# Attention and a softplus feed-forward on one core: products and TensorE sums issued for two key tiles at a time

## The chip, the cores and the metric

One core of a Trainium2 chip runs the whole program. The metric is device time in microseconds (us) from start to end of one execution; three runs of the kernel before gave 985.01, 985.25 and 985.94 us, median 985.25 us.

## The reference

For each of 4 batches and 8 heads there are 1152 keys and values of 64 numbers, and 576 queries, which are means of two neighbouring rows of `q`. Attention's output is the input of a two-layer feed-forward with a softplus between the layers.

```python
q_pool = q.reshape(B, H, S // 2, 2, D).mean(axis=3)
scores = scale * np.matmul(q_pool, k.transpose(0, 1, 3, 2))
attn = np.exp(scores - scores.max(-1)); attn /= attn.sum(-1) + 1e-09
x = np.matmul(attn, v)            # then (2304, 512): tokens by heads*64
h = x @ w_in                      # 512 -> 2048
g = np.maximum(h, 0.0) + np.log1p(np.exp(-np.abs(h)))
out = g @ w_out                   # 2048 -> 512
```

All of it is float32 at the ends. The kernel takes the large products of scores and feed-forward in float16 halves (a high part and a low part), and the product with the values and the sums of exponentials in float32.

## The kernel before

The work is cut into 16 units, `u0` to `u15`: a unit is one batch and two heads. A unit's 576 queries are taken in two halves, of 256 and 320 columns (`HALF`, `n`), and its 1152 keys in nine tiles of 128 (`KT`). For each half and each tile of keys, `attention` makes five kinds of work:

- **scores** (L777 and L780): four float16 matmuls, two for each head, into one of two PSUM buffers `s`;
- **exp** (L787): one ScalarE activation over both heads from `s` into one of four SBUF buffers `p`;
- **product** (L795): values times `p` for both heads into the one PSUM buffer `pv`. Each head takes 64 columns of the array. A float32 matmul of the program is two instructions in the trace, so one tile's product is 4 of them;
- **sums**: in units 0 to 5 (`SUMMED`) TensorE makes them (L802), with a matrix of ones and 32 columns of the array for each of four quarters, into the free end of `pv`, 8 instructions of the trace for one tile. In units 6 to 15 VectorE or GpSimd add the `p` tiles (L348) into `acc`, and TensorE sums over partitions once per half (`total`, L860);
- after the ninth tile: `pv` is copied out, the sums go through three small DMAs, `few`, `scratch` and `rinv` (L875, L880, L883), which turn them into one row of reciprocals for all partitions, and one multiplication finishes the half.

Ahead of a unit's attention, `maxima` computes its row maxima (L667 and L678 on TensorE, whose operands use 64 rows of the array, and reductions L688 on VectorE) and turns them (L713, L717). `feed_forward` does the first layer in blocks of columns (`unit`, L1009, then softplus on ScalarE, L1020), and the second layer in pieces of 12 matmuls (L960). Maxima, first and second layer share three PSUM buffers `m`.

The order of instructions on every engine is fixed when the program is built: each piece of work is a task with a price per engine, dependencies, a priority and buffers to take and give, and `Sched.run` plays the tasks through with those prices and lets each engine take the ready task of lowest priority number. On the chip, each engine then works in that order and waits where data isn't ready. In `attention` the scores of tile `kt` have priority `x.at + x.slow * (9 i + kt)`, the product that plus 1.9, the additions that plus 2.0. `ORDER` says which units and feed-forward blocks lie side by side: units 0 to 5 run nearly alone, from unit 6 on pieces of the second layer lie between attention's.

## Time and profile before

| | |
|---|---|
| median of three runs | 985.25 us |
| the profiled execution, its own time | 984.97 us |
| its span, first to last instruction | 983.3 us |
| TensorE (PE) busy | 903.1 us, 92% of the span |
| VectorE (DVE) busy | 608.3 us, 62% |
| ScalarE (ACT) busy | 472.4 us, 48% |
| GpSimd (POOL) busy | 162.8 us, 17% |
| mean granted TensorE clock | 0.979 of full speed |

Busy time is the union of an engine's instructions; a matmul's end is modelled, so what a block of matmuls takes is best read from the start of its first row to the start of the next row. A row of the timeline can hold several instructions (x8); its second column is how long they ran together. In brackets behind it stands how long the engine had been idle before, and who released it.

### The profile page before, as it was taken

To read this page: it belongs to the slowest core of one execution; us is meant where nothing else is said; L and a number is where in the kernel's file an instruction comes from. 1 tells how busy PE (TensorE), PEld (TensorE's weight loads), DVE (VectorE), ACT (ScalarE), POOL (GpSimd) and SP (SyncE) were. 2 spreads that over 40 slices of the span, in tenths; PEclk is the share of its full clock that TensorE was granted. 3 is DMA by queue.
4 is the path that set the end of the run, shared out by engine and by line. 5 is a ranking of instruction groups with operands and counts; after the bars stand their busy time and mean duration, and the time that the engine had idled before them with its cause. 6 is when DMAs were issued, how large, how long until landed. Compare 5 with 4: busy or idle time off the path is not lost.

```text
span 983.3 us, 16320 instructions
## 1 busy us (share of the span) xinstructions
PE 903.1 (92%) x6426; PEld 452.8 (46%) x6426; DVE 608.3 (62%) x1301; ACT 472.4 (48%) x739; POOL 162.8 (17%) x141
## 2 busy tenths in 40 slices
PE   2799999798789999999999999999899999969998
PEld 0244344244534456444544564333654744335483
DVE  5777587877667766666664467777654657526030
ACT  4547477777765345345442354455533545322020
POOL 1000010210212411134001112344112013000000
PEclk9999999799989999999999999999999999979999
DMA  8725426456434025041310151432300300000000
GB/s 239 189 81 152 124 78 190 115 170 162 123 94 104 12 62 90 12 136 37 68 37 28 43 96 39 107 78 68 86 1 17 91 1 17 13 18 1 22 12 21
DMA packets 101581, 74.61 MB, mean 76 GB/s; under 512 B 68480, under 2 KB 82816, under 8 KB 101504
## 3 DMA queue, kind: packets, MB, share of 16 engines
q1 hardware_dynamic: 101504, 73.57, 28.3%
q8 instruction: 50, 0.82, 0.4%
q14 instruction: 27, 0.22, 0.1%
HBM read 49.81 MB, written 4.79 MB: 56 GB/s over the span
## 4 chain that ended last, share of the span: by engine, by line
PE 54%; DMA 8%; DVE 7%; ACT 4%; issue 1%; POOL 0%; SPq 0%; ACTq 0%; DVEq 0%
PE m L960 16%; PE m L1009 14%; PE pv L795 10%; DMA rinv<-scratch 5%; PE s L777 5%; PE s L780 4%; PE m L667 3%; DVE nm L688 2%; DMA scratch<-few 2%; DMA few<-rinv 1%; ACT g L1020 1%; ACT p L787 1%; DVE xT L348 1%; ACT L787 1%; DVE w L275 1%
## 5 line engine op out<-in xcount | busy, mean ns | idle before, releaser
L787 ACT ACTIVATE p<-s,cols 128x512 f32<-128x512 f32 (+1 forms) x288 | 209.5, 738 | 209.3 <-PE s L780 206.8
L688 DVE TENSOR_REDUCE nm<-m 128x1 f32<-128x384 f32 x432 | 222.6, 550 | 108.9 <-PE m L667 100.3
L795 PE MATMUL pv<-p,v 128*64 128x320 f32 (+1 forms) x1152 | 207.1, 441 | 3.4 <-ACT rinv L868 1.6
L960 PE MATMUL m<-w,gh 128*128 128x512 f16 x576 | 171.8, 380 | 0.0
L777 PE MATMUL s<-qA,kT 128*128 128x256 f16 (+1 forms) x576 | 159.4, 296 | 8.5 <-ACT p L787 8.4
L780 PE MATMUL s<-qB,kB 66*128 66x256 f16 (+1 forms) x576 | 157.8, 293 | 0.0
L348 POOL TENSOR_TENSOR acc<-acc,p 128x512 f32<-128x512 f32 (+1 forms) x73 | 104.6, 1433 | 225.2 <-ACT p L787 189.8
L1009 PEld LDWEIGHTS <-w1h 128*128 128x128 f16 x1024 | 99.7, 99 | 49.7 <-issue 25.4
L960 PE MATMUL m<-w,gl 128*128 128x512 f16 x288 | 109.1, 379 | 0.0
L1020 ACT ACTIVATE g<-m,blk 128x512 f32<-128x512 f32 (+1 forms) x80 | 51.4, 642 | 110.1 <-PE m L1009 106.3
L1009 PE MATMUL m<-xh,w1h 128*128 128x256 f16 (+1 forms) x512 | 85.4, 289 | 17.7 <-DVE xh L272 7.7
L777 PEld LDWEIGHTS <-kT 128*128 128x128 f16 x576 | 57.8, 100 | 90.4 <-issue 80.6
L667 PE MATMUL m<-kT,qA 64*128 64x384 f16 x384 | 74.3, 347 | 20.2 <-DMA qA<-qcat 9.6
L795 PEld LDWEIGHTS pv<-p,v 128*64 128x64 f32 x1152 | 58.7, 137 | 72.2 <-issue 57.6
L960 PEld LDWEIGHTS <-gh 128*128 128x128 f16 x576 | 54.1, 98 | 68.0 <-issue 11.1
L1009 PE MATMUL m<-xl,w1h 128*128 128x256 f16 (+1 forms) x512 | 85.2, 290 | 0.0
L1009 PE MATMUL m<-xh,w1l 128*128 128x256 f16 (+1 forms) x512 | 84.8, 289 | 0.0
L348 DVE TENSOR_TENSOR acc<-acc,p 128x640 f32<-128x640 f32 (+1 forms) x67 | 50.8, 758 | 45.1 <-ACT p L787 36.9
L272 DVE TENSOR_SCALAR gh<-g,blk 128x512 f16<-128x512 f32 (+1 forms) x64 | 29.4, 459 | 76.4 <-ACT g L1020 76.1
L780 PEld LDWEIGHTS <-kB 66*128 66x128 f16 x576 | 57.3, 100 | 19.3 <-issue 9.3
L275 DVE SCALAR_TENSOR_TENSOR gl<-g,blk,gh 128x512 f16<-128x512 f32 (+1 forms) x80 | 55.7, 696 | 5.1 <-ACT gh L315 2.3
L667 PEld LDWEIGHTS <-qA 64*128 64x128 f16 x384 | 19.5, 93 | 85.2 <-issue 75.3
(139 smaller groups left out, 836.3 us busy)
## 6 DMA issues: line engine op xcount, KB each, us to landing
raw<-in_k_dram SPq DMA_DIRECT2D x16, 576.0 KB
v<-in_v_dram SPq DMA_DIRECT2D x16, 576.0 KB
raw<-in_q_dram SPq DMA_DIRECT2D x64, 128.0 KB
raw<-in_moe_w_out_dram SPq DMA_DIRECT2D x16, 512.0 KB
kB<-kT SPq DMA_DIRECT2D x32, 144.0 KB
gh<-in_moe_w_in_dram SPq DMA_DIRECT2D x4, 1024.0 KB
gl<-in_moe_w_in_dram SPq DMA_DIRECT2D x4, 1024.0 KB
out_dram<-o SPq DMA_DIRECT2D x16, 256.0 KB
```

The source lines that it names most:

```text
L272: nc.vector.tensor_scalar(out=out_, in0=in_, scalar1=s1, scalar2=s2, op0=op0, **kw)
L275: nc.vector.scalar_tensor_tensor(out=out_, in0=in0, scalar=s, in1=in1, op0=op0, op1=op1)
L348: e.tensor_tensor(out=o, in0=a, in1=b, op=op)
L667: nc.tensor.matmul(out=ps[h].item[:, 0:384], lhsT=x.qA.item[hs, PLACE[h, t]], rhs=x.kT.item[hs, k0:k0 + 3].rearrange("p a b -> p (a b)"), ...
L688: parts.append(task([("DVE", dve(384), lambda c=c, g=g, bank=bank: nc.vector.tensor_reduce(out=x.nm3.item[:, c, g:g + 1], in_=bank.item[:, ...
L777: nc.tensor.matmul(out=s.item[:, h, 0:n], lhsT=x.kT.item[:, h * KT + kt], rhs=x.qA.item.rearrange("p a b -> p (a b)")[:, c0:c0 + n], start ...
L780: nc.tensor.matmul(out=s.item[:, h, 0:n], lhsT=x.kB.item[0:D + 2, h * KT + kt], rhs=x.qB.item[0:D + 2, h, t0 * 64:t1 * 64], start=False, s ...
L787: nc.scalar.activation(out=pt.item[:, :, 0:n], in_=s.item[:, :, 0:n], func=ACTF.Exp, scale=x.sc)
L795: nc.tensor.matmul(out=pv.item[h * 64:(h + 1) * 64, 0:n], lhsT=x.v.item[:, h, kt], rhs=pt.item[:, h, 0:n], start=(kt == 0), stop=(kt == KT ...
L960: nc.tensor.matmul(out=ps.item[:, 0:512], lhsT=gt[:, f, t * 128:(t + 1) * 128], rhs=w2[:, f, wt, :], start=(f == 0 and m == 0), stop=(f == ...
L1009: nc.tensor.matmul(out=pv[:, f], lhsT=wt[:, kk, c0:c0 + 128], rhs=xt[:, kk, 0:w], start=(idx == 0), stop=(idx == 11))
L1020: x = task([("ACT", act(N, 1, 1), lambda: nc.scalar.activation(out=gs.item[:, 0:N], in_=ps.item[:, 0:N], func=ACTF.Softplus, scale=ih[:, g ...
```

## The change

The tiles of keys are put in five groups for each half: (0,1), (2,3), (4,5), (6,7) and (8). Scores and exp stay one task per tile, with the same buffers. The product is one task per group: it waits for both exponentials, then issues the sums of both tiles and the products of both tiles (products first in the group that begins at tile 0). Its priority is that of the group's first tile plus 2.8. The additions of units 6 to 15 get that priority too. Prices change: scores plus 60 instead of 30, products plus 220 or 140 per group instead of 160 or 80 per tile. In units 0 to 5 a `p` buffer now has one user to begin with, instead of two of which one is taken off at once.

```diff
--- before.py
+++ after.py
@@ -362,6 +362,7 @@
              "U6", "D6", "U7", "D7")
     SUMMED = range(6)
     STEPS = 2 * KT
+    GROUPS = [tuple(range(a, min(a + 2, KT))) for a in range(0, KT, 2)]
     blocks = []
     for b in range(B):
         if b % 2 == 0:
@@ -550,7 +551,7 @@
         x.kT, x.kB, x.qA, x.qB = (
             Hold(kT_r, 2 * KT + 15), Hold(kB_r, 2 * KT), Hold(qA_r, 2 * KT + 15), Hold(qB_r, 2 * KT))
         x.qlow = Hold(qlow_r, 3)
-        x.v = Hold(v_r, 2 * KT + 1)
+        x.v = Hold(v_r, 2 * len(GROUPS) + 1)
         x.sc = c[8]
 
 
@@ -765,69 +766,77 @@
         for i, (t0, t1) in enumerate(HALF):
             n = (t1 - t0) * 64
             pv, acc = Hold(pv_r), Hold(acc_r)
+            here = x.u in SUMMED
             before = None
             sums = None
-            for kt in range(KT):
-                prio = x.at + x.slow * (9.0 * i + kt)
-                s, pt = Hold(s_r), Hold(p_r, 2)
...
-                y = task([("PE", pe(4, n) + 30.0, scores)], [x.kB_done, x.q2_done, *x.qB_done[i]], prio, take=[s],
-                         give=[x.kT, x.kB, x.qA, x.qB])
...
-                e = task([("ACT", act(2 * n, 1, 1), exp)], [y, x.sc_done, *gate], prio, take=[pt], give=[s])
-                exps.setdefault(x.u, []).append(e)
...
-                def product_and_sums(kt=kt, product=product, summed=summed):
...
-                here = x.u in SUMMED
-                y = task([("PE", pe(1, (6 if here else 4) * n) + (160.0 if here else 80.0), product_and_sums if here else product)],
-                         [e, x.v_done], prio + 1.9,
-                         take=[pv] if kt == 0 else [], give=[pt, x.v])
...
-                    sums = task(tt_ways(2 * n, add, ALU.add), [e, before if kt == 1 else sums], prio + 2.0,
-                                take=[acc] if kt == 1 else [], give=[pt] + ([first] if kt == 1 else []))
-                    sums.price = {"DVE": 500.0}
-                before = e
+            first = done = None
+            for group in GROUPS:
+                prio = x.at + x.slow * (9.0 * i + group[0])
+                items = [(kt, Hold(s_r), Hold(p_r, 1 if here else 2)) for kt in group]
+                es = []
+                y = None
+                for kt, s, pt in items:
+                    def scores(kt=kt, s=s, t0=t0, t1=t1, n=n, i=i):
+                        for h in range(2):
+                            c0 = FIRST[h, i]
+                            nc.tensor.matmul(out=s.item[:, h, 0:n], lhsT=x.kT.item[:, h * KT + kt],
+                                             rhs=x.qA.item.rearrange("p a b -> p (a b)")[:, c0:c0 + n],
+                                             start=True, stop=False)
+                            nc.tensor.matmul(out=s.item[:, h, 0:n], lhsT=x.kB.item[0:D + 2, h * KT + kt],
+                                             rhs=x.qB.item[0:D + 2, h, t0 * 64:t1 * 64], start=False, stop=True)
+
+                    y = task([("PE", pe(4, n) + 60.0, scores)], [x.kB_done, x.q2_done, *x.qB_done[i]],
+                             x.at + x.slow * (9.0 * i + kt), take=[s], give=[x.kT, x.kB, x.qA, x.qB])
+
+                    def exp(s=s, pt=pt, n=n):
+                        nc.scalar.activation(out=pt.item[:, :, 0:n], in_=s.item[:, :, 0:n], func=ACTF.Exp,
+                                             scale=x.sc)
+
+                    es.append(task([("ACT", act(2 * n, 1, 1), exp)], [y, x.sc_done, *gate], prio, take=[pt],
+                                   give=[s]))
+                exps.setdefault(x.u, []).extend(es)
+
+                def products(items=items, pv=pv, n=n):
+                    for kt, _, pt in items:
+                        for h in range(2):
+                            nc.tensor.matmul(out=pv.item[h * 64:(h + 1) * 64, 0:n], lhsT=x.v.item[:, h, kt],
+                                             rhs=pt.item[:, h, 0:n], start=(kt == 0), stop=(kt == KT - 1))
+
+                def summed(items=items, pv=pv, n=n):
+                    for _, _, pt in items:
+                        for a in range(2):
+                            for h in range(2):
+                                g = 64 * h + 32 * a
+                                nc.tensor.matmul(
+                                    out=pv.item[g:g + 32, 512 - n // 2:512], lhsT=ones[:, 0:32],
+                                    rhs=pt.item[:, h, a * n // 2:(a + 1) * n // 2], start=False, stop=False,
+                                    tile_position=(0, g))
+
+                def products_and_sums(group=group, products=products, summed=summed):
+
+                    for part in (products, summed) if group[0] == 0 else (summed, products):
+                        part()
+
+                m = len(group)
+                y = done = task([("PE", pe(m, (6 if here else 4) * n) + (220.0 if here else 140.0),
+                           products_and_sums if here else products)],
+                         es + [x.v_done, done], prio + 2.8,
+                         take=[pv] if group[0] == 0 else [], give=[o[2] for o in items] + [x.v])
+                if here:
+                    sums = y
+                else:
+                    for (kt, _, pt), e in zip(items, es):
+                        if kt == 0:
+                            first, before = pt, e
+                            continue
+
+                        def add(kt=kt, acc=acc, pt=pt, first=first, n=n):
+                            a = acc.item[:, :, 0:n]
+                            return a, (first.item[:, :, 0:n] if kt == 1 else a), pt.item[:, :, 0:n]
+
+                        sums = task(tt_ways(2 * n, add, ALU.add), [e, before if kt == 1 else sums], prio + 2.8,
+                                    take=[acc] if kt == 1 else [], give=[pt] + ([first] if kt == 1 else []))
+                        sums.price = {"DVE": 500.0}
             prio = x.at + x.slow * (9.0 * i + KT)
             c0 = t0 * 64
             homes = [(place(b, p, c0 + o, c0 + o + m), slice(o, o + m), wait)
```

On TensorE, unit 0, second half: the scores of tile 4, then the sums and products. `kT0`, `kB0`, `qA0`, `qB0` and `v0` belong to unit 0, `kT1` and `qA1` to unit 1, whose maxima (L667, L668 in the changed kernel) lie between; `p3`, `p0` hold tiles 2 and 3. Before:

```order
L780 MATMUL s1_106<-qB0_88,kB0_81 128x320
L802 MATMUL pv0_107<-p0_90,ones_111 32x160 x4
L795 MATMUL pv0_107<-p0_90,v0_76 64x320 x2
L667 LDWEIGHTS qA1_87
L667 MATMUL m0_108<-kT1_80,qA1_87 128x384
L667 LDWEIGHTS qA1_87
L667 MATMUL m1_109<-kT1_80,qA1_87 128x384
L777 LDWEIGHTS kT0_79
L777 MATMUL s0_105<-qA0_86,kT0_79 128x320
L780 LDWEIGHTS kB0_81
```

The changed kernel at the same place:

```order
L785 MATMUL s1_106<-qB0_88,kB0_81 128x320
L810 MATMUL pv0_107<-p3_93,ones_111 32x160 x4
L810 MATMUL pv0_107<-p0_90,ones_111 32x160 x4
L802 MATMUL pv0_107<-p3_93,v0_76 64x320 x2
L802 MATMUL pv0_107<-p0_90,v0_76 64x320 x2
L668 LDWEIGHTS qA1_87
L668 MATMUL m0_108<-kT1_80,qA1_87 128x384
L668 LDWEIGHTS qA1_87
L668 MATMUL m2_110<-kT1_80,qA1_87 128x384
L782 LDWEIGHTS kT0_79
L782 MATMUL s0_105<-qA0_86,kT0_79 128x320
```

The sums and the product of tile 2, which stood ahead of the scores of tile 4, have moved behind them, next to those of tile 3.

On TensorE, unit 2, first half, around the scores of tile 4 (in `s0`), which follow those of tile 3 (in `s1`). Before:

```order
L780 MATMUL s1_106<-qB0_88,kB0_81 128x256
L802 MATMUL pv0_107<-p2_92,ones_111 32x128 x4
L795 MATMUL pv0_107<-p2_92,v0_76 64x256 x2
L777 LDWEIGHTS kT0_79
L777 MATMUL s0_105<-qA0_86,kT0_79 128x256
L780 LDWEIGHTS kB0_81
```

The changed kernel, from the second head of tile 4's scores on:

```order
L782 LDWEIGHTS kT0_79
L782 MATMUL s0_105<-qA0_86,kT0_79 128x256
L785 LDWEIGHTS kB0_81
L785 MATMUL s0_105<-qB0_88,kB0_81 128x256
L668 LDWEIGHTS qA0_86
L668 MATMUL m0_108<-kT0_79,qA0_86 128x384
L668 LDWEIGHTS qA0_86
L668 MATMUL m2_110<-kT0_79,qA0_86 128x384
L782 LDWEIGHTS kT0_79
L782 MATMUL s1_106<-qA0_86,kT0_79 128x256
```

Scores of tiles 3, 4 and 5 now follow each other with one pair of maxima between them; the third of them writes `s1` again, which the exp of tile 3 has to have read.

On TensorE, the end of unit 15, the last one: `total` (L860, in the changed kernel L869), the last product, and then the first layer of the last wide block (L1009, now L1018). Before:

```order
L960 MATMUL m0_108<-w2_63,gl_65 128x512
L860 MATMUL m2_110<-acc1_95,ones_111 32x160 x4
L795 MATMUL pv0_107<-p0_90,v1_77 64x320 x2
L960 LDWEIGHTS gh_64
L960 MATMUL m0_108<-w2_63,gh_64 128x512
```

Eleven more matmuls of L960 follow there, then the first layer. The changed kernel:

```order
L785 MATMUL s1_106<-qB1_89,kB1_82 128x320
L802 MATMUL pv0_107<-p1_91,v1_77 64x320 x2
L802 MATMUL pv0_107<-p2_92,v1_77 64x320 x2
L802 MATMUL pv0_107<-p3_93,v1_77 64x320 x2
L869 MATMUL m0_108<-acc1_95,ones_111 32x160 x4
L1018 LDWEIGHTS w1h_61
L1018 MATMUL m1_109<-xh_70,w1h_61 128x384
```

The last piece of the second layer that lay behind `total` has moved ahead of it, and the last product too.

## Rows read from the trace of the kernel before

**Rows 1.** The page's head and its part 1: busy time, share of the span and instructions of each engine.

```profile
span 983.3 us, 16320 instructions
...
PE 903.1 (92%) x6426; PEld 452.8 (46%) x6426; DVE 608.3 (62%) x1301; ACT 472.4 (48%) x739; POOL 162.8 (17%) x141
```

**Rows 2.** Busy time by stretches: the stretch in us from the span's start, its length, busy time and instructions of each engine, the granted clock, the DMA engines' share, GB/s.

```profile
0.00:45.00 45.00, 20.16 (x90) 7.56 (x90) 31.57 (x58) 21.75 (x32) 4.93 (x10) 1.00 0.84 226
45.00:175.00 130.00, 124.37 (x1160) 54.22 (x1153) 92.34 (x224) 81.74 (x130) 5.85 (x8) 0.97 0.45 125
175.00:200.00 25.00, 19.00 (x137) 7.22 (x136) 21.18 (x46) 20.77 (x38) 6.48 (x6) 0.80 0.45 116
200.00:225.00 25.00, 23.99 (x236) 10.73 (x236) 19.42 (x49) 18.72 (x36) 3.38 (x3) 1.00 0.50 164
225.00:275.00 50.00, 37.35 (x310) 25.72 (x311) 33.97 (x77) 40.41 (x65) 7.74 (x8) 0.95 0.49 129
275.00:862.00 587.00, 569.50 (x3873) 284.79 (x3874) 378.42 (x788) 268.11 (x410) 133.91 (x105) 0.99 0.23 56
```

**Rows 3.** Timeline of TensorE in unit 0, second half (start in us, how long, line, operation, x instructions).

```profile
59.69 0.75 PE L802 MATMUL pv<-p,ones 128*32 128x160 f32 x16
60.37 0.76 PE L795 MATMUL pv<-p,v 128*64 128x320 f32 x4
61.06 0.34 PE L667 MATMUL m<-kT,qA 64*128 64x384 f16 x2
61.33 0.31 PE L777 MATMUL s<-qA,kT 128*128 128x320 f16 x1
...
61.75 0.30 PE L780 MATMUL s<-qB,kB 66*128 66x320 f16 x1
61.98 0.48 PE L802 MATMUL pv<-p,ones 128*32 128x160 f32 x8
62.39 0.76 PE L795 MATMUL pv<-p,v 128*64 128x320 f32 x4
```

**Rows 4.** The same view at the places where blocks of two tiles happened to meet: sums and products of 256 columns near 119 us, two products of 320 columns at 645 us, and two of 256 at 672 us.

```profile
118.63 0.64 PE L802 MATMUL pv<-p,ones 128*32 128x128 f32 x16
119.21 0.65 PE L795 MATMUL pv<-p,v 128*64 128x256 f32 x4
119.79 0.28 PE L777 MATMUL s<-qA,kT 128*128 128x256 f16 x1
...
120.34 0.43 PE L802 MATMUL pv<-p,ones 128*32 128x128 f32 x8
120.69 0.65 PE L795 MATMUL pv<-p,v 128*64 128x256 f32 x4
...
645.12 1.30 PE L795 MATMUL pv<-p,v 128*64 128x320 f32 x8
646.35 0.34 PE L667 MATMUL m<-kT,qA 64*128 64x384 f16 x2
...
672.00 1.08 PE L795 MATMUL pv<-p,v 128*64 128x256 f32 x8
673.01 0.34 PE L667 MATMUL m<-kT,qA 64*128 64x384 f16 x2
```

**Rows 5.** The same view where scores are followed by the second layer.

```profile
847.37 0.30 PE L780 MATMUL s<-qB,kB 66*128 66x320 f16 x1
...
847.51 0.59 PE L960 MATMUL m<-w,gh 128*128 128x512 f16 x2
```

**Rows 6.** Groups of instructions by line with shapes apart: busy us, mean ns of one, idle us before and what ended it.

```profile
L787 ACT ACTIVATE p<-s,cols 128x640 f32<-128x640 f32 x144 | 112.8, 792 | 113.3 <-PE s L780 111.6 <-DVE nm L688 1.4
...
L795 PEld LDWEIGHTS pv<-p,v 128*64 128x64 f32 x1152 | 58.7, 137 | 72.2 <-issue 57.6 <-ACT p L787 7.0 <-ACT rinv L868 2.1
...
L315 ACT ACTIVATE qcat<-raw,cols 128x1152 f16<-128x1152 f32 x16 | 19.9, 1243 | 2.2 <-DVE cols L292 2.2
```

**Rows 7.** Timeline near 100 us: the last score matmul of a tile, and the exp that reads it.

```profile
100.17 0.30 PE L780 MATMUL s<-qB,kB 66*128 66x320 f16 x1
...
100.51 0.79 ACT L787 ACTIVATE p<-s,cols 128x640 f32<-128x640 f32 x1 [2.98 <-PE s L780]
```

**Rows 8.** TensorE's waits between 45 and 862 us: who waited for whom, us in total, times, the longest.

```profile
PE s L777 <- ACT p L787: 8.4, 7, 4.5
...
PE pv L795 <- ACT rinv L868: 1.6, 1, 1.6
```

**Rows 9.** The sums' line alone (L802) in the three early stretches where TensorE is not full: PE and PEld busy with the number of instructions, granted clock, DMA.

```profile
0.00:45.00 45.00, 1.65 (x24) 0.61 (x24) 1.00 0.84 226
175.00:200.00 25.00, 3.94 (x56) 1.21 (x56) 0.80 0.45 116
225.00:275.00 50.00, 2.40 (x40) 0.79 (x40) 0.95 0.49 129
```

**Rows 10.** Timeline of TensorE at the end of unit 15.

```profile
860.31 0.48 PE L860 MATMUL m<-acc,ones 128*32 128x160 f32 x8
...
861.41 0.60 PE L960 MATMUL m<-w,gh 128*128 128x512 f16 x2
...
864.01 0.65 PE L1009 MATMUL m<-xh,w1h 128*128 128x384 f16 x3
872.38 0.48 PE L1009 MATMUL m<-xh,w1h 128*128 128x384 f16 x1 [7.72 <-DVE xh L272]
```

29 lines of the change are left out of this document (removed).

## The prediction

> **What bounds the kernel now.** I read the page's busy shares first: TensorE is busy 903.1 of 983.3 us, the next engine, VectorE, 62% [rows 1]. An average over stages decides nothing, so the windows came next [rows 2]. From 45 to 175 us TensorE works 124.4 of 130 us, from 200 to 225 us 24.0 of 25, from 275 to 862 us 569.5 of 587. There, time taken from TensorE is time taken from the kernel. It isn't so before 45 us (20.2 of 45), from 175 to 200 (19.0 of 25) and from 225 to 275 us (37.4 of 50). Third, the timeline, read from the start of one row to the start of the next. In unit 0 one tile's sums take 62.39 - 61.98 = 0.41 us and its product 61.06 - 60.37 = 0.69; its scores take 61.98 - 61.33 = 0.65, a pair of maxima 0.27 [rows 3].
>
> **What a block costs beyond its matmuls.** The trace of before already holds blocks of two tiles, where two happened to meet, and so the price of pairing.
> - Products of 320 columns: one tile 0.69 [rows 3], two in a row 646.35 - 645.12 = 1.23 [rows 4]. Apart they cost 1.38; pairing saves 0.15. Of 256 columns: 0.58 alone, 1.01 for two, saving 0.15 [rows 4].
> - Sums: 0.41 alone, 60.37 - 59.69 = 0.68 for two [rows 3], saving 0.14; in the half of 256 queries 0.35 and 0.58 [rows 4], saving 0.12. I take 0.13.
> - Scores: the last score matmul before sums takes 61.98 - 61.75 = 0.23 [rows 3]; before the second layer, which uses the array in the same shape, 847.51 - 847.37 = 0.14 [rows 5]. Leaving scores for a block of another shape costs 0.09.
>
> The price is paid where one shape of the array follows another, whatever lies ahead.
>
> The Trainium skill has a rule that speaks against the change: in "TensorE: Matmul & The Clock Gate", Part 3, "The mechanism", it says that a weight load overlaps with running matmuls only if it goes to another group of rows. Both tiles' products use all 128 rows, so by this rule the second tile's loads would stand open. The rows say otherwise: the second tile adds 1.23 - 0.69 = 0.54 us, less than the first tile took, so nothing of its loads is open. By the rule the sum would end on the other side; it is the fifth case below.
>
> **The change, part by part.** It removes no arithmetic and adds none. Counted over the whole order of TensorE, unbroken blocks of products fall from 281 to 159 (not from 288 to 160: some tiles met already), blocks of sums from 105 to 60, and score blocks that are followed by another shape from 218 to 153. So:
> - products: 122 x 0.15 = 18.3 us
> - sums: 45 x 0.13 = 5.9 us
> - scores: 65 x 0.09 = 5.9 us
>
> Together 30.1 us less TensorE work. Maxima stay 186 blocks (185), the feed-forward keeps its blocks. Exponentials, additions and DMAs stay in number; some 14 casts leave ScalarE for the others, which I cost at nothing, as ScalarE is busy 48% [rows 1].
>
> What comes off this:
> - *Stretches that TensorE doesn't bound.* There lie 24 + 56 + 40 = 120 instructions of sums [rows 9], at 8 a tile 15 tiles, or 15 x 4/9 = 6.7 of the 48 pairs of units 0 to 5. Each would save 0.15 + 0.13 + 0.09 = 0.37; 2.5 us are not paid out.
> - *The last unit.* From `total` of unit 15 to the first layer that needs its result, 872.38 - 860.31 = 12.07 us pass: copy, three DMAs, multiplication, cast. Before, the last product (0.69) and a piece of the second layer (864.01 - 861.41 = 2.60) run in that time; TensorE then idles 7.72 [rows 10]. In the changed order both lie ahead of `total`. They cost no more there, but the cover is gone: 3.3 us, idle about 11.
> - *Scores that come early.* A score block needs its `s` buffer read by the exp two tiles back. That exp starts 0.04 us after the scores' end (100.51 against 100.47 [rows 7]) and takes 0.79 [rows 6]: 0.83. Before, sums and products lay between. Now at 25 places (3 before) three score blocks stand in a row, with a pair of maxima or less between: cover 0.65 + 0.27 = 0.92. That is just enough while ScalarE does nothing else; with another job ahead, TensorE waits for it, and everything behind waits too, the maxima for VectorE included. The longest usual job is 1.24 us [rows 6]. So each of the 22 new places costs from nothing to 1.24 us, 0 to 27 us together. Below nothing is possible too: before, scores already wait 8.4 us for exps [rows 8], and another order may lose those. ScalarE is busy 63% from 45 to 175 us and 46% from 275 to 862 us [rows 2], its exps among that; I take 0.25 a place, near the lower end as most of ScalarE's jobs are the exps themselves: 5.5 us.
> - *Change of half.* The next half's first product waits until `pv` is copied out. Between the last product of one half and the first of the next, the order leaves 0.8 to 0.9 us at three places in units 1, 2 and 5 where it left about 1.6. The one such wait of before is 1.6 us [rows 8]; from 0 to 1.6 a place, I take 0.5, 1.5 us.
> - *Products that wait for two exps.* Nearly everywhere the next tile's scores or more lie between, so that the second exp's 0.83 us is covered; I cost it at nothing. Without that cover it would be up to 0.83 for each of 128 pairs.
> - *The `p` ring.* A pair takes two of four buffers and gives them back together. The exp of tile 4 needs the pair (0,1) done, which the order puts ahead of tile 5's scores or earlier: nothing.
>
> Sum: 30.1 - 2.5 - 3.3 - 5.5 - 1.5 = 17.3 us. Against the span: 983.3 - 17.3 = 966.0; around the span lie 984.97 - 983.3 = 1.7 us, so 967.7 for the profiled execution, and the median of the runs is 0.3 above it: 968.
>
> **The rivals.**
> 1. *All of it arrives.* The new order has no more waits than the old one, but for the last unit: 30.1 - 3.3 = 26.8, 958.5 us. For it: the prices of the changed tasks come nearer to what a pair takes, so waits of before may go. Against: covers got shorter at 22 places.
> 2. *A second bound in units 0 to 5.* VectorE is busy 92.3 of 130 us from 45 to 175, 21.2 of 25 from 175 to 200, ScalarE 40.4 of 50 from 225 to 275 [rows 2]. If preparing the next unit already sets the pace there, the 48 x 0.37 = 17.8 us of these units are lost: 30.1 - 17.8 - 3.3 - 2.8 (half of the early scores) = 6.2, 979 us. Against: from 45 to 175 us TensorE has 96%.
> 3. *Slower: ScalarE's other jobs stand in front of the early scores.* If each of the 22 places pays 1.24 us, 27.3 us go, with the other three losses of 7.3 more than the gain: 30.1 - 34.6 = -4.5, 990 us. It decides from (30.1 - 7.3) / 22 = 1.04 us a place on. For it: before, one such wait was 4.5 us [rows 8]. Against: that was 1 of 7, the others share 3.9.
> 4. *Nothing comes of it*: the order shifts everywhere, and waits of other kinds eat the gain; 985.
> 5. *Weight loads stand open in the merged blocks.* A product's load takes 0.137 us [rows 6], two after one another for each merged tile (the heads' run side by side): 122 x 0.27 = 33, so 17.3 - 33 = -16, 1001 us. Against: the 1.23 us of rows 4.
>
> **How the numbers follow.** Forecast 0.52, first rival 0.20, second 0.13, third 0.08, fourth 0.05, fifth 0.02. Under 0.2%, 2 us, this kernel's measurement doesn't tell a change from none. Faster: 0.52 + 0.20 + 0.13 = 0.85; same 0.05; slower 0.10. The range goes from below the first rival, for waits that vanish, to no change: 955 to 985, leaving out the slower cases and a little below.
>
> **What would show it.** In the changed profile, products should come in blocks of x8 at 1.23 or 1.01 us and sums as x16 at 0.68 or 0.58; TensorE's busy time should fall by about 30 us to some 873. Its wait for `xh` at the end should read about 11 us instead of 7.7. The scores' waits for exp should grow from 8.4 to about 14 us; if they grow by over 23, the third rival holds. Units 0 to 5 should end about 14 us earlier; if not, and VectorE is over 90% busy there, the second holds. The forecast is wrong if TensorE's busy time falls by much less than 30 us, or if its idle time grows by more than that.

## The result and the profile after

The changed kernel takes 995.85 us (median of four runs, 993.42 to 997.34) against 985.32 us of the kernel before on the same chip: ratio 1.0101, 95% interval 1.0061 to 1.0141. It is 1% slower. The forecast was 968, with a range of 955 to 985: the time and its sign were both missed.

The page's head, part 1 and the first line of its chain of waits, of the kernel after; they answer to [rows 1]:

```profile
span 993.8 us, 16332 instructions
...
PE 884.5 (89%) x6426; PEld 476.6 (48%) x6426; DVE 620.3 (62%) x1312; ACT 456.9 (46%) x718; POOL 166.5 (17%) x151
...
PE 60%; DMA 16%; DVE 12%; ACT 7%; issue 2%; SPq 2%; POOL 1%; ACTq 0%; DVEq 0%; POOLq 0%
```

TensorE's busy time fell by 903.1 - 884.5 = 18.6 us, and yet the span grew by 10.5. Busy shares don't show why: VectorE stands at 62% as before. The first hint is the chain: DMA makes 16% of it, where it was 8% of the kernel before's, a chain that covers only 74% of its span. The same stretches as in [rows 2], after:

```profile
0.00:45.00 45.00, 18.66 (x80) 7.46 (x80) 31.74 (x59) 21.48 (x31) 4.48 (x10) 1.00 0.80 212
45.00:175.00 130.00, 112.29 (x1076) 57.19 (x1074) 92.31 (x221) 78.06 (x125) 7.47 (x9) 0.92 0.46 125
175.00:200.00 25.00, 20.74 (x187) 9.51 (x187) 19.53 (x43) 20.22 (x34) 1.32 (x3) 0.93 0.45 138
...
275.00:862.00 587.00, 555.88 (x3831) 297.93 (x3830) 384.45 (x800) 254.68 (x392) 138.71 (x112) 0.97 0.22 56
```

From 45 to 175 us TensorE was busy 124.4 us before and is 112.3 now, with fewer instructions in the stretch (1076 for 1160): it stands. The granted clock fell with it, from 0.97 to 0.92, and from 0.99 to 0.97 in the long stretch. VectorE is fullest from 175 to 200 us, with 19.5 of 25 us, 78%.

The blocks did what the prediction said. Timeline of TensorE, unit 0, second half, after (answers to [rows 3, 4]):

```profile
58.18 1.30 PE L802 MATMUL pv<-p,v 128*64 128x320 f32 x8
59.41 0.75 PE L810 MATMUL pv<-p,ones 128*32 128x160 f32 x16
60.09 0.34 PE L668 MATMUL m<-kT,qA 64*128 64x384 f16 x2
```

Start to start, two products take 59.41 - 58.18 = 1.23 us and two tiles' sums 60.09 - 59.41 = 0.68. By one sentence of the Trainium skill ("TensorE: Matmul & The Clock Gate", Part 3, "The mechanism"), that weight loads overlap with running matmuls only if the group of rows differs, the second tile's loads would stand open, since both tiles use the same rows of the array. The trace doesn't agree with that sentence: the second tile adds 0.54 us where the first takes 0.69. The same section leaves room for what the trace shows, as it excepts loads that go to the array's background weight buffer.

To account for all of TensorE's time I summed, over each trace's timeline, the time from a block's start to the next block's start less the idle time in brackets. That splits the span into work by kind and idle:

| | before | after | difference |
|---|---|---|---|
| products, sums, scores | 404.6 | 384.0 | -20.6 |
| all else (maxima, feed-forward, transposes, totals, the end) | 505.3 | 508.5 | +3.2 |
| idle between blocks | 73.4 | 101.3 | +27.9 |

A block takes longer where the granted clock is lower, so these differences hold two things. The clock records of both traces tell them apart, if each block's time is multiplied by the clock it was granted. At full speed products, sums and scores fall by 394.9 - 365.2 = 29.7 us and all else grows by 1.9; running below full speed costs 16.1 us before and 26.4 after, 10.3 more. In this account the 27.8 us less work at full speed are just what the new idle time takes, and the 10.5 us of loss are about what the clock costs.

The idle time, by who was waited for (kernel after, the whole span: who waits and for whom, us in total, times, the longest; [rows 8] show the same view of 45 to 862 us):

```profile
PE m L668 <- DVE nm L689: 20.0, 16, 3.2
PE s L782 <- ACT p L792: 11.9, 11, 4.5
PE m L1018 <- DVE xh L272: 11.2, 1, 11.2
PE m L1018 <- ACT g L1029: 9.6, 13, 1.9
...
PE m L284 <- ACT gh L438: 6.3, 1, 6.3
```

The first of them in the kernel before:

```profile
PE m L667 <- DVE nm L688: 7.2, 9, 1.5
```

The wait for `xh` is the 7.72 us of [rows 10], the one for `gh` was not there. No single row holds the 28 us, and they name several engines. Three places show a cause that they share. Timeline of the kernel after near 138 us (start, how long, engine, line; in brackets the idle time ahead and its releaser):

```profile
125.52 0.18 DVE L887 RECIPROCAL few<-few 128x5 f32<-128x5 f32 x1
126.51 0.46 SPq L889 DMA_DIRECT2D scratch<-few  x1
131.89 0.58 SPq L892 DMA_DIRECT2D rinv<-scratch  x1
138.17 0.42 DVE L348 TENSOR_TENSOR xT<-xT,rinv 128x256 f32<-128x256 f32 x1 [2.87 <-DMA rinv<-scratch]
138.52 1.34 DVE L275 SCALAR_TENSOR_TENSOR raw<-gh,raw 128x1024 int32<-128x1024 int32 x1
139.78 0.80 DVE L275 SCALAR_TENSOR_TENSOR qlow<-raw,cols,qcat 128x576 f16<-128x576 f32 x1
140.51 2.41 DVE L424 TENSOR_TENSOR raw<-raw,gh 128x1024 f32<-128x1024 f32 x1
142.96 1.12 ACT L438 ACTIVATE gh<-raw 128x1024 f32<-128x1024 f32 x1 [7.53 <-DVE raw L424]
144.21 0.59 PE L284 MATMUL m<-amw,ones 128*128 128x1 f32 x2 [6.28 <-ACT gh L438]
```

The multiplication that ends a half waits at the head of VectorE's queue for the row of reciprocals. All that is queued behind it is late, among it the `raw` that ScalarE waits 7.53 us for, and so TensorE stands 6.28 us in a row that names ScalarE. At most 2.87 of these 6.28 us are the row's; the rest is VectorE's own work ahead of `gh`, 2.41 us of it L424. A second place, near 448 us, names yet another wait, the scores' for exp:

```profile
447.57 0.49 DVE L348 TENSOR_TENSOR xT<-xT,rinv 128x320 f32<-128x320 f32 x1 [5.51 <-DMA rinv<-scratch]
448.10 0.61 ACT L315 ACTIVATE xh<-xT,blk 128x384 f16<-128x384 f32 x1 [5.75 <-DVE xT L348]
448.62 1.35 ACT L792 ACTIVATE p<-s,cols 128x512 f32<-128x512 f32 x2
449.34 0.43 PE L782 MATMUL s<-qA,kT 128*128 128x320 f16 x1 [4.52 <-ACT p L792]
```

The 5.51 us pass through VectorE and ScalarE, where the exp is queued behind the cast `xh`, to TensorE. A third, near 688 us, is the longest of the waits for `nm`:

```profile
687.93 0.43 DVE L348 TENSOR_TENSOR xT<-xT,rinv 128x256 f32<-128x256 f32 x1 [4.33 <-DMA rinv<-scratch]
...
688.40 1.01 DVE L689 TENSOR_REDUCE nm<-m 128x1 f32<-128x384 f32 x2
689.01 0.78 PE L668 MATMUL m<-kT,qA 64*128 64x384 f16 x2 [3.25 <-DVE nm L689]
```

Not every wait is of this kind: at 660 us TensorE stands 2.64 us for `nm` behind VectorE's own work, whose last piece takes 2.08 us, with no wait for the row just ahead. How often VectorE stands for this row, before and after, by the view of waits:

```profile
DVE xT L348 <- DMA rinv<-scratch: 44.6, 24, 7.9
```

```profile
DVE xT L348 <- DMA rinv<-scratch: 55.1, 19, 8.1
```

The wait was there before; now it takes 2.9 us each time instead of 1.9. GpSimd, which makes 11 of the changed kernel's 40 multiplications, stands for the row too, 88.8 us for `xT` and 14.5 for `xm`. And a stand of TensorE costs more than itself. Slices of 4 us around the first place, kernel after (TensorE busy, granted clock, DMA share, GB/s):

```profile
136.00:140.00 4.00, 1.92 (x26) 1.00 0.57 155
140.00:144.00 4.00, 0.00 (x0) 0.54 0.00 0
144.00:148.00 4.00, 3.79 (x26) 0.50 0.52 142
148.00:152.00 4.00, 4.00 (x24) 0.68 0.40 153
152.00:156.00 4.00, 4.00 (x53) 1.00 0.41 129
```

The clock fell to its lower level, 1.2 GHz, in the empty slice, and TensorE then worked at 0.50 and 0.68: 3.79 x 0.50 + 4.00 x 0.32 = 3.2 us more went after a stand of 6.3.

### The profile page after: what moved, and what is told of

Its sections match the earlier page's. It is cut to its first block, busy times and chain, and to the rows that moved or that the text cites. A ratio compares the mean times of both kernels' runs of the same rounds, so it can differ in the third digit from the quotient of the medians.

```text
span 993.8 us, 16332 instructions
## 1 busy us (share of the span) xinstructions
PE 884.5 (89%) x6426; PEld 476.6 (48%) x6426; DVE 620.3 (62%) x1312; ACT 456.9 (46%) x718; POOL 166.5 (17%) x151
## 4 chain that ended last, share of the span: by engine, by line
PE 60%; DMA 16%; DVE 12%; ACT 7%; issue 2%; SPq 2%; POOL 1%; ACTq 0%; DVEq 0%; POOLq 0%
PE m L969 16%; PE m L1018 13%; PE pv L802 11%; DMA rinv<-scratch 8%; PE s L782 6%; PE s L785 5%; PE m L668 4%; DVE nm L689 3%; DMA scratch<-few 3%; PE pv L810 2%; DMA raw<-in_moe_w_out_dram 2%; ACT p L792 2%; DVE kcat L275 2%; DVE w L275 1%; DVE acc L348 1%
## 5 line engine op out<-in xcount | busy, mean ns | idle before, releaser
L792 ACT ACTIVATE p<-s,cols 128x512 f32<-128x512 f32 (+1 forms) x288 | 204.7, 737 | 214.3 <-PE s L785 210.2
L802 PE MATMUL pv<-p,v 128*64 128x320 f32 (+1 forms) x1152 | 185.0, 439 | 1.0 <-ACT rinv L877 0.4
L782 PE MATMUL s<-qA,kT 128*128 128x256 f16 (+1 forms) x576 | 159.4, 297 | 12.3 <-ACT p L792 11.9
L348 POOL TENSOR_TENSOR acc<-acc,p 128x512 f32<-128x512 f32 (+1 forms) x67 | 100.2, 1495 | 238.4 <-ACT p L792 139.9
L1018 PEld LDWEIGHTS <-w1h 128*128 128x128 f16 x1024 | 100.1, 99 | 59.2 <-issue 35.1
L1018 PE MATMUL m<-xh,w1h 128*128 128x256 f16 (+1 forms) x512 | 85.4, 289 | 26.8 <-DVE xh L272 11.2
L668 PE MATMUL m<-kT,qA 64*128 64x384 f16 x384 | 77.3, 348 | 34.2 <-DVE nm L689 20.0
L802 PEld LDWEIGHTS pv<-p,v 128*64 128x64 f32 x1152 | 71.0, 141 | 71.4 <-issue 41.8
L1018 PE MATMUL m<-xl,w1h 128*128 128x256 f16 (+1 forms) x512 | 85.5, 290 | 0.0
L1018 PE MATMUL m<-xh,w1l 128*128 128x256 f16 (+1 forms) x512 | 84.8, 289 | 0.0
L272 DVE TENSOR_SCALAR gh<-g,blk 128x512 f16<-128x512 f32 (+1 forms) x65 | 29.7, 458 | 76.2 <-ACT g L1029 76.0
L348 DVE TENSOR_TENSOR acc<-acc,p 128x512 f32<-128x512 f32 (+1 forms) x73 | 55.1, 754 | 28.1 <-ACT p L792 18.5
L668 PEld LDWEIGHTS <-qA 64*128 64x128 f16 x384 | 19.9, 93 | 88.5 <-issue 78.4
```

Of the source, the lines that this page charges most:

```text
L272: nc.vector.tensor_scalar(out=out_, in0=in_, scalar1=s1, scalar2=s2, op0=op0, **kw)
L348: e.tensor_tensor(out=o, in0=a, in1=b, op=op)
L668: nc.tensor.matmul(out=ps[h].item[:, 0:384], lhsT=x.qA.item[hs, PLACE[h, t]], rhs=x.kT.item[hs, k0:k0 + 3].rearrange("p a b -> p (a b)"), ...
L782: nc.tensor.matmul(out=s.item[:, h, 0:n], lhsT=x.kT.item[:, h * KT + kt], rhs=x.qA.item.rearrange("p a b -> p (a b)")[:, c0:c0 + n], start ...
L792: nc.scalar.activation(out=pt.item[:, :, 0:n], in_=s.item[:, :, 0:n], func=ACTF.Exp, scale=x.sc)
L802: nc.tensor.matmul(out=pv.item[h * 64:(h + 1) * 64, 0:n], lhsT=x.v.item[:, h, kt], rhs=pt.item[:, h, 0:n], start=(kt == 0), stop=(kt == KT ...
```

## The experiments

Three questions: is it the pairs or the new order; is it VectorE's work; is it the row. Theories are named in the expectations by letters. Two remained: D, VectorE's own work is a second bound, and L, a latency that doesn't shrink (the row's two DMAs) stands at the head of an in-order queue, and a shorter TensorE runs into it. All ratios are against the kernel before on the same chip, with 95% intervals.

**Where the pairs are.** Pairs in a part of the units, single tiles with the prices and priorities of before in the rest (e1: units 6 to 15 paired; e2: units 0 to 5 paired); in e3 the changed code, with its prices and priorities, and groups of one everywhere. The diff is e1's.

```diff
+    SINGLES = [(t,) for t in range(KT)]
...
+        return GROUPS if u >= 6 else SINGLES
...
-            for group in GROUPS:
...
+            for group in groups_of(x.u):
```

> Pairs with the changed prices and priorities in units 6 to 15 only; units 0 to 5 as before. By blocks 16.0 us less TensorE work. In the trace of the changed kernel units 6 to 15 lost 11 us against before in spite of that. Theory P: the loss belongs to the pairs of these units, so it comes again: 993 to 998 us. Theory W: it belonged to one order of many; this one is laid out anew, 970 to 992 us, and the places of the largest waits differ from those of the changed kernel.

> Pairs with the changed prices and priorities in units 0 to 5 only; units 6 to 15 priced as before. By blocks 14.1 us less TensorE work. In the trace of the changed kernel the sums of unit 5 were ready 1.2 us earlier than before, so that 13 us of the saving was eaten by waits there. Theory P: 983 to 986 us. Theory W: 970 to 995 us, with the largest waits at other places than in the changed kernel.

> The changed kernel with groups of one tile: its prices and its priorities (plus 2.8), but no pairs, so no saving in blocks (281 to 287 blocks of products). Theory W: the planner lays out another order, and that alone moves the time by several us either way; 980 to 1000 us, if above 988 the new priorities and prices are part of the loss. Theory P: without pairs nothing is lost, 984 to 987 us.

Measured: e1 994.59 us, ratio 1.0124 (1.0076 to 1.0173); e2 984.14, 0.9999 (0.9973 to 1.0025); e3 983.90, 1.0010 (0.9982 to 1.0037). The new priorities and prices without pairs change nothing. With pairs in the early units the work of products, sums and scores falls by 404.6 - 395.9 = 8.7 us and nothing comes out; in the late units it falls by 9.7 and the kernel is 1.2% slower. Theory P's times came true in e1 and e2, and in e3 to within 0.1 us.

**Pairs in the order of before.** The plan, prices and priorities of before; an even tile's product and sums are only issued together with the next tile's.

```diff
+                    held.append((product, summed if here else None))
+                    if kt % 2 == 0 and kt < KT - 1:
+                        return
```

> The kernel before, with its own planned order, prices and priorities; only the product (and, in units 0 to 5, the sums) of an even tile is issued together with that of the next tile. On TensorE unbroken blocks of products fall from 281 to 160, of sums from 105 to 60, scores followed by another shape from 218 to 180: 27.4 us less work by the same prices as in the prediction. Theory W (the pairs themselves pay, the waits come from the new order that the planner lays out around them): 957 to 968 us, TensorE's waits between 45 and 862 us about as before (some 40 us). Theory P (a pair as such lacks slack: it waits for two exponentials and gives its buffers back late): 980 to 1000 us, with the waits of scores and products for exponentials grown by 10 us or more.

Measured: 979.31 us, 0.9963 (0.9935 to 0.9992). Products, sums and scores take 379.1 us, 25.5 less than before, but idle grows from 73.4 to 85.4 and the rest of the work by 7.3. The time lies between the two theories' ranges. A little of the gain arrives, far less than was expected if the order were all: pairs in either order run into something. It isn't P's lack of slack towards the exponentials: the scores' waits for exp grew by 3.1 us, from 8.4 to 11.5, and not by 10.

**Honest prices.** The changed kernel with scores plus 100 and pairs plus 305 or 155, as the trace has them.

```diff
+            s_cost, h_cost, n_cost, p_late, a_late = (100.0, 305.0, 155.0, 2.8, 2.8) if paired else (60.0, 220.0, 140.0, 2.8, 2.8)
...
-                    y = task([("PE", pe(4, n) + 60.0, scores)], [x.kB_done, x.q2_done, *x.qB_done[i]],
+                    y = task([("PE", pe(4, n) + s_cost, scores)], [x.kB_done, x.q2_done, *x.qB_done[i]],
...
-                y = done = task([("PE", pe(m, (6 if here else 4) * n) + (220.0 if here else 140.0),
+                y = done = task([("PE", pe(m, (6 if here else 4) * n) + (h_cost if here else n_cost),
```

> The changed kernel with prices as the traces have them: scores plus 100, a pair's products and sums plus 305, products alone plus 155 (for a pair of 320 columns 1.91 and 1.23 us). All else as changed. Theory D: the planner now places maxima and scores at the times at which they can go; a part of the waits goes, 970 to 985 us. Theory S: 990 to 998 us.

Measured: 988.89 us, 1.0014 (0.9979 to 1.0049); idle still 90.2. Better than the changed kernel, level with before, and just under theory S's range.

**Is it VectorE's work?** The maxima's reductions read 96 of 384 columns (this leaves out three quarters of each row when its maximum is taken); VectorE's largest group falls from 222 to 94 us. On before (f1), after (f2) and the order kept (f3):

```diff
-                            out=x.nm3.item[:, c, g:g + 1], in_=bank.item[:, 0:384], axis=AX.X, op=ALU.max,
+                            out=x.nm3.item[:, c, g:g + 1], in_=bank.item[:, 0:96], axis=AX.X, op=ALU.max,
```

> The kernel before, but each reduction for the row maxima reads 96 of its 384 columns: three quarters of the keys are left out of the maxima, and VectorE gets some 130 us less work (432 reductions of about 250 instead of 550 ns); order and prices are unchanged. This is the base for the two kernels beside it. Theory D (where TensorE waits, it waits for VectorE, which has to keep up with its reductions): the waits of the maxima and of what hangs on them go, 960 to 975 us. Theory S (the pairs lack slack towards the exponentials on ScalarE): nothing much, 978 to 985 us.

> The changed kernel with the same lighter reductions for the maxima (three quarters of the keys left out of them). Theory D: now the 30 us that pairing takes from TensorE arrive, 15 to 30 us below the lighter kernel before (about 940 to 955 us). Theory S: the pairs lose as much as ever, 3 to 13 us above the lighter kernel before.

> The kernel with pairs in the order of the kernel before, with the same lighter reductions (three quarters of the keys left out of the maxima). Theory D: 20 to 27 us below the lighter kernel before. Theory S: 3 to 8 us below it, as with the full reductions.

Measured: f1 975.56, 0.9882 (0.9817 to 0.9947); f2 975.26, 0.9881 (0.9821 to 0.9941); f3 963.41, 0.9752 (0.969 to 0.9814). With some 130 us less work on VectorE the changed kernel draws level but doesn't gain, and it still idles 94.9 us (f1: 71.0). Pairing brings 23.9 us of new idle here instead of 27.9. Against f1 both theories missed twice: f2 is level, and f3 is 12.2 us below, between S's 3 to 8 and D's 20 to 27. VectorE's work has a part in the loss; it isn't the cause alone.

**Is it the row?** The multiplication takes a constant instead of the row; the DMAs are issued all the same, and the plan is the same. Each sum's reciprocal is replaced by 1/1152.

```diff
-                task(tt_ways(cs.stop - cs.start, lambda dst=dst, cs=cs, ri=ri: (dst, dst, ri.item[:, cs]),
+                task(tt_ways(cs.stop - cs.start, lambda dst=dst, cs=cs, ri=ri: (dst, dst, flat[:, 0:1].to_broadcast([128, cs.stop - cs.start])),
```

> The kernel before, with one thing left out: the multiplication that ends a half takes a constant 1/1152 for every sum's reciprocal instead of the row `rinv`, so it no longer stands at the head of VectorE's queue until the two DMAs scratch<-few and rinv<-scratch (some 12 us after one another) are through. The DMAs are still issued and the plan is unchanged. Theory L (latencies that don't shrink stand at the head of an in-order queue, and a shorter TensorE runs into them): in the kernel before TensorE is mostly longer than they are; -1 to -8 us, ratio 0.992 to 0.999, VectorE's waits for rinv (8.2 us from 45 to 300) gone. Theory D (VectorE's own work is the second bound): 0 to -2 us.

> The changed kernel with the same constant in the place of the reciprocals. Theory L: VectorE's waits for rinv (16.1 us from 45 to 300 us) go, with them TensorE's 6 us stand at 144 us (behind ScalarE's gh, behind VectorE's raw, behind that wait) and part of its 20 us for nm; -15 to -25 us, 971 to 981 us, idle of TensorE from 101 to below 85, and the gap to the kernel before with the same constant falls from +10.5 to between 0 and -10. Theory D: -2 to -4, the gap stays near +8. Rival O (the changed order itself puts work late on TensorE, whatever the latencies are): the gap to the kernel before stays near +10.

> Pairs in the order of the kernel before (e5), with the same constant. Theory L: this kernel has the shortest TensorE and gains at least as much: -8 to -20 against e5, 960 to 971 us, 15 to 25 below the kernel before with the constant. Theory D: level with e5, within 3 us (977 to 982).

> The changed kernel with both reliefs: the constant for the reciprocals, and maxima reductions that read 96 of 384 columns (leaves out three quarters of each row of scores when the maximum is taken). If D and L between them hold the whole of the idle time that the change brought, TensorE's idle falls to about 70 us (68 to 78), the granted clock to 0.98, and the time to 950 to 962 us. If it stays at 970 or more with over 90 us idle, most of the new idle time has another cause, in the order itself (O).

> The kernel before with both reliefs (constant for the reciprocals, maxima reductions that read 96 of 384 columns), beside the changed kernel with both (h4: 0.9515 of the kernel before, 941 us). If the row and VectorE between them were all that ate the gain, pairs are worth their block savings here, 20 to 27 us: this is 961 to 968 us, ratio 0.975 to 0.98. If the changed order loses time by itself (O), the gap is under 10 us: 943 to 951, ratio 0.955 to 0.964.

| kernel | us | ratio (interval) | products, sums, scores | idle |
|---|---|---|---|---|
| h1: before, constant | 965.40 | 0.9768 (0.9692 to 0.9843) | 401.7 | 58.2 |
| h2: after, constant | 955.87 | 0.9656 (0.9594 to 0.9718) | 376.2 | 71.4 |
| h3: order kept, constant | 954.33 | 0.9648 (0.9587 to 0.971) | 378.3 | 69.7 |
| i1: before, constant and 96 columns | 957.15 | 0.9683 (0.9636 to 0.9731) | 400.7 | 58.7 |
| h4: after, constant and 96 columns | 941.33 | 0.9515 (0.9452 to 0.9578) | 373.6 | 69.3 |

Times are medians; work and idle are those of the profiled execution, which for h1 was its fastest (960.66 us).

This separates the theories. Taking the row's wait away brings the changed kernel 1.0101 - 0.9656 = 0.0445 of the time of before, and the kernel before 1 - 0.9768 = 0.0232, and the sign turns: 10.5 us slower becomes 9.5 us faster. D had asked for -2 to -4 us in h2; it got -40. O had asked for a gap that stays near +10; and h2 and h3, the changed order and the order kept, are level once the row is away. L's expectations held in direction, but most of its sizes were off: -40 instead of -15 to -25 in h2, in h1 -20 instead of -1 to -8, and h3 is 11.1 us below h1 instead of 15 to 25. The kernel before lost much to the row too. The constant doesn't make the multiplication itself shorter: on VectorE those of `xT` took 607 ns on the mean before and 631 in h1, 500 after and 566 in h2. Some 8 us of each fall are the last unit's chain, which the constant cuts as well (the wait for `xh` is 3.0 us in h2 and gone in h1). TensorE's waits in h2, where the 6.3 us for `gh` are gone and those for `xh`, `nm` and exp are smaller than in the changed kernel:

```profile
PE m L669 <- DVE nm L690: 14.6, 15, 2.6
...
PE s L783 <- ACT p L793: 7.2, 9, 2.1
...
PE m L1019 <- DVE xh L273: 3.0, 1, 3.0
```

In h1 the scores' wait for exp is the longer one:

```profile
PE s L778 <- ACT p L788: 10.3, 7, 6.4
```

With both reliefs pairs are worth 957.15 - 941.33 = 15.8 us (on two chips; by the ratios 0.0168 of the time of before): between what the two theories of that expectation gave. h4's idle, 69.3, is as expected if D and L hold all of it, and its time is below the range given for that. 27.1 us of work go, and 10.6 us of idle come. The rows that differ most, i1 and then h4:

```profile
PE s L778 <- ACT p L788: 10.8, 7, 6.6
...
PE m L668 <- DVE nm L689: 9.1, 6, 6.7
PE m L1010 <- ACT g L1021: 6.1, 9, 1.7
```

```profile
PE m L669 <- DVE nm L690: 11.5, 11, 6.3
PE s L783 <- ACT p L793: 9.8, 12, 2.1
...
PE m L1019 <- ACT g L1030: 8.8, 13, 1.9
PE m L285 <- DVE few L888: 3.5, 1, 3.5
PE m L1019 <- DVE xh L273: 3.0, 1, 3.0
```

So the idle time that pairing brings is 27.9 us as it stands, 23.9 with lighter reductions, 71.4 - 58.2 = 13.2 with the constant, and 10.6 with both. The row holds about half of it.

**The same, computing the reference.** Why does the multiplication stand at the head? In the plan's table of lags, the time from the reciprocals' end to the row is 5.56 us: 1.40 from VectorE to the DMA `scratch<-few`, 0.30 as its price, 2.30 to the next DMA, 0.60 as the price of `rinv<-scratch`, 0.96 back to VectorE.

```python
        "DVE": {"DVE": 40.0, "ACT": 45.0, "POOL": 60.0, "PE": 55.0, "DMA": 1400.0},
...
        "DMA": {"DVE": 960.0, "ACT": 960.0, "POOL": 960.0, "PE": 960.0, "DMA": 2300.0},
```

In the rows near 138 us it took 138.17 - 125.70 = 12.5 us, near 448 us 12.0 (its reciprocal ended at 435.57); over the 20 times that VectorE stood for it in the changed kernel (the 19 shown above for `xT`, and one for `xm`), 6.6 to 13.4; over the 24 in the kernel before, 6.6 to 18.9. Some of it is the wait to be issued: near 214 us the reciprocal ended at 213.91 and the first DMA was issued at 217.50. So the plan puts the multiplication into VectorE's queue where it takes the row to be there, up to 8 us too early. I added 3.5 us to that lag and nothing else:

```diff
-                            u.ready[x] = max(u.ready[x], free[e] + self.LAG[e].get(x, 150.0))
+                            u.ready[x] = max(u.ready[x], free[e] + t.lag + self.LAG[e].get(x, 150.0))
...
+            y.lag = 3500.0
```

> The kernel before; the plan alone takes the row of reciprocals to arrive 3.5 us later than it did (some 5.5 us after the reciprocals' end as planned, 6.6 to 13 as measured), so that the multiplication is put further back in VectorE's or GpSimd's queue. Nothing is left out. If the latency costs because the plan has it too short (L): VectorE's waits for rinv fall from 44.6 us to under 15, and the time by 3 to 12 us, ratio 0.988 to 0.997. If the order of the rest decides: 0.998 or more.

> Pairs issued in the manner of e5 (each even tile's product and sums held until the next tile's), with the plan's row 3.5 us later. Nothing is left out. Theory L: -6 to -18 against e5, 962 to 974 us, and faster than both kernels of the case. If the order decides: within 4 us of e5 (976 to 984).

> The changed kernel with the plan's row 3.5 us later. Nothing is left out. Theory L: VectorE's waits for rinv fall from 55 us to under 20, TensorE's idle from 101 to 75 to 90, time 970 to 985 us. If the order decides: 990 to 1000.

| kernel | us | ratio (interval) | products, sums, scores | idle |
|---|---|---|---|---|
| j0: before, row later | 969.87 | 0.9805 (0.9752 to 0.9858) | 400.2 | 63.7 |
| j1: order kept, row later | 960.31 | 0.9707 (0.966 to 0.9753) | 373.6 | 72.0 |
| j2: after, row later | 962.87 | 0.9737 (0.9693 to 0.978) | 374.9 | 75.7 |

All three fell at least as far as L's most hopeful end. The page's head of j2, and VectorE's wait for the row in it, of which 8.2 us are the end of the last unit:

```profile
span 960.6 us, 16326 instructions
...
PE 877.6 (91%) x6426; PEld 475.3 (49%) x6426; DVE 614.2 (64%) x1303; ACT 461.4 (48%) x724; POOL 166.8 (17%) x154
```

```profile
DVE xT L348 <- DMA rinv<-scratch: 11.9, 3, 8.2
```

From 55.1 to 11.9 us. Five of the 40 multiplications moved from VectorE to GpSimd in j2; in j0, where one moved the other way, VectorE's wait fell as well, from 44.6 to 10.2. GpSimd's wait hardly changed in j2, 95.2 us for 103.3, so j2's gain isn't owed to it. j1 and j2 beat both kernels of the case; with a plan that knows the row's latency, pairs gain 969.87 - 962.87 = 7.0 us in the changed kernel, 9.6 in the order kept. A caution: the plan moves instructions everywhere, so a part of each fall could be another order's luck. Against luck speaks that each of the three fell by some four fifths of what the constant brought it: 0.0195 of 0.0232, 0.0256 of 0.0315, 0.0364 of 0.0445.

**The last unit, and prices once more.** j2 with single tiles in unit 15, so that its last product and a piece of the second layer stand behind `total` again (j3); j2 with e4's prices (j4).

> The changed kernel with the plan's row 3.5 us later, pairs in units 0 to 14 only. Unit 15 goes by single tiles, and the order puts its last product and a piece of the second layer behind `total` again, as in the kernel before. If the prediction's term for the last unit holds: the wait for xh falls from 11.4 to about 8, the wait behind unit 15 is 3.3 us shorter; unit 15's own pairs are given up (about 18 tiles in 8 pairs, some 2 us more TensorE work), so 961 to 964 us against 962.9, level. If the clock falls in the long wait and costs beyond it, the end gets 5 us or more shorter.

> The changed kernel with the prices as measured (e4: scores plus 100, pairs plus 305 or 155) and the plan's row 3.5 us later. If the prices were a fault of their own, they add to the latency's gain: 950 to 959 us. If the latency was what mattered and e4's gain came from the same waits: 960 to 968, level with 962.9.

Measured: j3 959.98 us, 0.9744 (0.9676 to 0.9812); j4 963.85, 0.9784 (0.9728 to 0.984). TensorE's timeline at the first layer behind unit 15, j2 and j3:

```profile
850.82 0.48 PE L1019 MATMUL m<-xh,w1h 128*128 128x384 f16 x1 [11.36 <-DVE xh L272]
```

```profile
849.46 0.48 PE L1026 MATMUL m<-xh,w1h 128*128 128x384 f16 x1 [7.34 <-DVE xh L272]
```

The cover is worth 11.36 - 7.34 = 4.0 us there; in the whole time, given what unit 15's own pairs save, it can't be told from nothing. Honest prices add nothing to the honest latency: what e4 had won back is inside what the latency wins.

## Why the prediction was wrong, point by point

- *The blocks: right.* 1.23 and 0.68 us were foretold and came. Of the 30.1 us, 29.7 came at full speed. At the clock that was granted it was 20.6 in the changed kernel, where stretches at the lower clock lengthen the same blocks, and 25 to 27 where the change brings fewer of them (j0 to j2: 400.2 - 374.9 = 25.3; i1 to h4: 27.1).
- *The step that failed* is the list of what comes off. It has the normalisation's chain ("copy, three DMAs, multiplication, cast") in the item on the last unit alone, as a cost where TensorE itself waits for its end, once. The same chain runs 32 times, and VectorE stands for it, 44.6 us before. I read TensorE's waits [rows 8] and the busy shares, and priced no wait on VectorE, since it was only 62% busy. A queue that stands is not busy, and everything behind it stands too. In place of the 12.8 us that were to come off, 27.9 us of idle and 3.2 of other work took back the blocks' 20.6 and 10.5 more. With the row's wait removed that loss turns into a gain, and pairing brings 13.2 us of idle (h1 to h2) or 12.0 (j0 to j2): about half of the 27.9 was the row's.
- *The list has no term for the clock either*: 10.3 us more than before went to TensorE's work below full speed. Three long stretches at the lower level begin inside stands, those near 140, 448 and 880 us.
- *The rule by which I read the windows was wrong in its second half*: "time taken from TensorE is time taken from the kernel" needs the other queues' fixed latencies to be covered by more than what is taken. TensorE at 96% from 45 to 175 us didn't say that they were: over the whole span, the kernel before already got 2.3% faster when the row's wait was taken from it (h1).
- *Last unit, 3.3 us*: right. The wait for `xh` went from 7.72 to 11.23 us, +3.5; put back, 4.0.
- *Scores that come early, 5.5 us*: not confirmed. The scores' wait for exp grew by 3.5 us with the change (8.4 to 11.9), and its longest, 4.52, came through the row. Out of the row's way it grew by 6.9 from j0 (2.2) to j2 (9.1), but fell by 3.1 from h1 to h2 and by 1.0 from i1 to h4.
- *Change of half, 1.5 us*: it cost nothing; from 45 to 862 us the waits of `pv` for the copy `rinv` fell from 1.6 us to 0.7. *Products that wait for two exps, nothing*: right; the waits of `pv` for exp fell from 2.8 us to 0.6.
- *Casts that leave ScalarE, nothing*: VectorE is busy 620.3 - 608.3 = 12.0 us longer. No run takes this away by itself; in h2 VectorE is busy 13.4 us longer than in h1, and the pairs gain all the same.
- *Stretches that TensorE doesn't bound, 2.5 us*: early pairs brought nothing at all while the row stood (e2); how much of that was lost in these stretches isn't shown. With the row relieved the early units end 7.8 us (h1 to h2) and 8.0 us (j0 to j2) earlier.
- *Rivals.* The second came nearest in place (the early units ended 1.2 us earlier instead of 14, by the issue of their last `few`), but not in cause: it asked for VectorE over 90% busy, which was 71% from 45 to 175 us and 78% in its fullest stretch. The third asked for ScalarE's jobs before the early scores to take over 23 us more; they took 3.5. The fourth spoke of "waits of other kinds", which is what came, but gave it 0.05 and no loss. The fifth fell with the 1.23 us. No rival had a DMA's latency in a queue, and none had the clock.
- *The diagnostics* worked: the forecast was to be wrong if busy time fell by much less than 30 us and if idle grew by more than that. Busy fell by 18.6, and 27.9 of idle ate it.

What stays open: in the cleanest pair (i1 and h4) 10.6 us of new idle remain. Their rows name it: `few` 3.5, `xh` 3.0, `g` +2.7, `nm` +2.4, scores -1.0. Why these waits come with pairs was not followed. From j0 to j2 it is the scores' 6.9 and the 3.5 for `xh`, of 12.0.

## What to carry to other kernels

Before making the busiest engine shorter, list the waits of every in-order queue that feeds it, the idle ones too, and above all those that end with a DMA: a latency at the head of a queue doesn't shrink with the work, and it reaches the busy engine under other engines' names. Where an order is planned with assumed latencies, compare the assumed one with the trace first; here that correction alone was worth 2% (j0), and only with it did the changed kernel beat the one before (j2).

## What was not expected of the hardware

- Two DMAs in a chain, of 2 to 2.5 and 128 to 160 KB, took 6.6 to 13.4 us from the reciprocals' end to the multiplication, the wait to be issued included. At the six stands before 300 us it was 8.6 to 13.4, where the DMA engines are busy 0.45 to 0.62 from 45 us on; at the six from 720 us on, 6.6 to 8.1. The Trainium skill ("DMA: Bandwidth & Descriptors", "Anatomy of one DMA — SWDGE (gpsimd) path") gives about 2.0 us fixed for a DMA on another path; the rows near 138 us have 5.4 and 6.3 us for the two.
- What a stand costs behind itself: 3.2 us of lower clock after 6.3 us without a matmul. Over the span the mean granted clock fell from 0.979 to 0.964 with the change, and the work below full speed cost 26.4 us instead of 16.1. In the four runs of h1 the mean was 0.975 to 0.989, in the seven of the kernel before beside them 0.966 to 0.981.
- "PSUM — Partial Sum Buffer", section "Engine vs sequencer instructions", of the Trainium skill says that the queues of ScalarE, VectorE and GpSimd are strictly first in, first out. The trace agrees: behind the 2.87 us stand at 138 us nothing of VectorE's passed, and a stand of 5.51 us on it became 5.75 on ScalarE and 4.52 on TensorE.
